# Sorting matrices of batches 1 to 3 built on VectorE, two heads at a time, instead of on GpSimd

## The chip, the cores and the metric

The kernel runs on one core of a Trainium2 chip. A core has TensorE (PE in the profile) for matrix products, VectorE (DVE), ScalarE (ACT) and GpSimd (POOL) for elementwise work, SyncE (SP), which here only issues transfers, and 16 DMA engines between its memory (SBUF) and the chip's main memory. PE writes to a second, small memory, PSUM, from which VectorE or ScalarE must copy its results. The metric is the device time of one execution in microseconds (us).

## The reference

Two stages are chained: a block-sorting attention, and a feed-forward network on its output. Shapes: q, k and v are 4 batches x 8 heads x 768 tokens x 64; `sort_net` has an 8 x 8 matrix for each batch and head.

```python
P = sort_net
for _ in range(5):
    P = exp(P - max(P, -1));  P = P / sum(P, -1);  P = P / sum(P, -2)
k_sorted = einsum('bhij,bhjcd->bhicd', P, k_blocks)     # 8 blocks of 96 tokens
v_sorted = einsum('bhij,bhjcd->bhicd', P, v_blocks)
attn = softmax(q_blocks @ k_sorted_blocks.T / 8)        # inside each block only
x = (attn @ v_sorted_blocks)  ->  3072 tokens x 512
h = maximum(x @ w_in, 0)                                # 512 -> 2048
out = (h * h) @ w_out                                   # 2048 -> 512
```

So each sorted block is a mixture of the head's 8 blocks, with the weights of one row of P.

## The kernel before

**Loads.** All inputs come through transfers that GpSimd issues (line 212), each of which converts to bf16: first the parts of batch 0, then the weights `w_in` and `w_out` in four quarters each, then q, k and v of batch 1 in two halves of four heads. The loads of batches 2 and 3 stand behind PE's last reads of batches 0 and 1, whose buffers they take.

**Sorting matrices.** The 768 tokens of a head lie on 128 partitions with 6 tokens each, so that a block is 16 partitions. The mixture of blocks is then a matrix product with a 128 x 128 matrix: P of the head, each entry spread over a 16 x 16 diagonal. These matrices of all 32 heads lie in `w_all` (128 partitions, 32 heads x 8 x 16, bf16). `build_w` (lines 323 to 335) writes those of `n` heads in one instruction, as the product of a 0/1 mask and the entries of P that `pt` holds, spread over the partitions (128 x 8 x 32). The entries of all batches are there once the Sinkhorn steps are done, at about 14 us. The eight heads of batch 0 are built on VectorE in three instructions (lines 621, 624, 625). The heads of batches 1 to 3 are built on GpSimd, with one instruction of eight heads for each batch (lines 626 and 627).

**Attention.** A unit of work is two heads of one batch; batch 0 is done in two halves of four blocks, the others whole. The stages of a unit: `s_q` transposes q on PE (line 361); `s_sort` makes the sorted K and then V as products with `w_all` (403), which are copied from PSUM by ScalarE or VectorE (line 166 or 168, tiles `ksT` and `vsT`); `s_sc` makes the scores (439) and their exponentials on ScalarE (455); `s_vt` transposes the sorted V (472), copied to `vs`; `s_av` makes the product of exponentials and V (499), which VectorE divides by the sums (508, 509); `s_xt` transposes the result (531) into `xT`, the network's input.

**Network.** Eight units of 384 tokens: 16 chunks of the up-projection (562), each with a ReLU on ScalarE (570) and a square on VectorE (573), then 12 chunks of the down-projection (590; four for each block of 128 tokens), each block copied and stored (605, 606).

**Order.** The order of the instructions on PE, VectorE and ScalarE is fixed ahead of time by a planner in the kernel's own program (`Plan`, lines 43 to 108). Each operation has an estimated cost, a list of operations that it depends on, and for attention on PE a due time, counted in network chunks. The planner goes through time, and takes for each engine what can start first; on equal terms it takes what was added first, and the network's operations are added last. Copies from PSUM may go to ScalarE or VectorE, whichever ends earlier by the estimates. PE has two queues, attention and network, and takes network chunks where the attention is not due or not ready. The planner's dependences order the instructions; on the chip an instruction waits only for the data that it uses. GpSimd's instructions keep the planner's order as well. Rotating PSUM slots (`Ring`, lines 26 to 40) limit how far PE runs ahead: two slots for sorts, scores and products with V together, three for the network, one for the transposes.

Of the kernel before, what the change touches and what calls it, by code (L numbers as in the profile page):

```python
# [111 lines left out]
def kernel(  # L112
# [10 lines left out]
    nc = tc.nc  # L123

    B, H, S, D = q.shape
# [27 lines left out]
    plan = Plan()  # L153
# [4 lines left out]
    def cost_f(n):  # L158
        return (0.17 + 0.82e-3 * n, 0.15 + 1.04e-3 * n)
# [4 lines left out]
    def copy(eng, out, in_):  # L164
        if eng == "ACT":
            nc.scalar.copy(out=out, in_=in_)  # L166
        else:
            nc.vector.tensor_copy(out=out, in_=in_)  # L168
# [89 lines left out]
    pt = const.tile([128, NB, NH], BF16)  # L258
# [61 lines left out]

    built = {}

    def build_w(h0, n, src, dep, eng="DVE"):
        def fn(e):
            s = tiles["pt"] if src is None else src
            (nc.gpsimd if eng == "POOL" else nc.vector).tensor_tensor(
                out=w_all[:, h0:h0 + n, :, :],
                in0=mask[:, None, None, :].to_broadcast([128, n, NB, C0]),
                in1=s[:, :, h0:h0 + n].rearrange("p i h -> p h i")[:, :, :, None]
                .to_broadcast([128, n, NB, C0]),  # L330
                op=ALU.mult)
        op = plan.add(eng, 0.15 + 0.134 * n, fn, [dep])
        for h in range(h0, h0 + n):
            built[h] = op
        return op
# [15 lines left out]
    def s_q(b, hp, p0, p1, due=0, after=None):  # L351

        n = p1 - p0
        t = {}

        def mm(e):
            qb = qkv[b][0]
            t["p"] = ps1.tile([128, NA, n], BF16, tag="p1", name="qtp")
            for a in range(NA):
                for h in range(2):  # L360
                    nc.tensor.transpose(  # L361
                        out=t["p"][64 * h:64 * (h + 1), a, :],
                        in_=qb[p0:p1, 2 * hp + h, D * a:D * (a + 1)],
                        identity=ident[p0:p1, p0:p1])
            if p0 == 0:
                tiles["qT", b, hp] = att.tile(
                    [128, NB, NA, C0], BF16, tag="qT", name="qT", bufs=6)

        def ev(e):
            copy(e, tiles["qT", b, hp][:, p0 // C0:p1 // C0, :, :],  # L370
                 t["p"].rearrange("p a (i c) -> p i a c", c=C0))

        if b == 0:
            dep = landed[b, 0, 0, p0]
        else:
            dep = landed[b, 0, HP * (2 * hp // HP), 0]
        s1, old = r1.take()
        if p0 == 0:
            qTs[b, hp], oldq = rqT.take()
        else:  # L380
            oldq = []
        pe = plan.add("PE", 0.1 + 0.002 * n, mm, [dep, after, id_op] + old, due)
        readers[b].append(pe)
        op = plan.add(AD, cost_b(NA * n), ev, [pe] + oldq)
        r1.use(s1, pe, op)
        rqT.use(qTs[b, hp], op)
        return op

    def s_sort(u, t, due=0, early=False):

        st = {}

        def mm(e):
            src = qkv[u.b][t]
            if early:
                tp = psf.tile([128, 512], FP32, tag="pf", name="tp")
                tp = tp[:, 0:NA * u.ni * C0].rearrange("p (a x) -> p a x", a=NA)
            else:
                tp = ps2.tile([128, NA, u.ni * C0], FP32, tag="p2", name="tp")
            st["p"] = tp  # L400
            for a in range(NA):
                for h in range(2):
                    nc.tensor.matmul(  # L403
                        out=tp[64 * h:64 * (h + 1), a, :],
                        lhsT=src[:, 2 * u.hp + h, D * a:D * (a + 1)],
                        rhs=w_all[:, H * u.b + 2 * u.hp + h, u.i0:u.i0 + u.ni, :]
                        .rearrange("p i c -> p (i c)"),
                        start=True, stop=True)

        def ev(e):  # L410
            h0 = u.halves[0]
            copy(e, (u.ksT if t == 1 else u.vsT)[:, h0:h0 + len(u.halves), 0:HS]
                 .rearrange("p h (x a) -> p h x a", a=NA),
                 st["p"].rearrange("p a (h x) -> p h x a", x=NQ * C0))

        h0 = 2 * u.hp
        dep = landed[u.b, t, h0 if u.b == 0 else HP * (h0 // HP), 0]
        ring = rf if early else r2
        s2, old = ring.take()
        pe = plan.add("PE", 0.385 if u.full else 0.27, mm,  # L420
                      [dep, built[H * u.b + h0], built[H * u.b + h0 + 1]] + old, due)
        readers[u.b].append(pe)
        op = plan.add(AD, cost_f(NA * C0 * u.ni), ev, [pe] + u.old)
        ring.use(s2, pe, op)
        return op

    def s_sc(u, due=0):

        u.exps = {}
        u.et, last = {}, []  # L430
        for hf in u.halves:
            st = {}

            def mm(e, hf=hf, st=st):
                qT = tiles["qT", u.b, u.hp]
                st["p"] = scp = ps2.tile([128, 2, 512], FP32, tag="p2", name="scp")
                for n in range(NQ):
                    for h in range(2):
                        nc.tensor.matmul(  # L439
                            out=scp[:, h, BLK * n:BLK * (n + 1)],  # L440
                            lhsT=u.ksT[64 * h:64 * (h + 1), hf, BLK * n:BLK * n + 128],
                            rhs=qT[64 * h:64 * (h + 1), NQ * hf + n, :, :]
                            .rearrange("p a c -> p (a c)"),
                            start=True, stop=True)

            s2, old = r2.take()
            u.et[hf], olde = ret.take()
            pe = plan.add("PE", 0.25, mm, [u.k_op, u.q_op] + old, due)
            r2.use(s2, pe)
            rqT.use(qTs[u.b, u.hp], pe)  # L450
            last.append(pe)
            u.exps[hf] = []
            for h in range(2):
                def ex(e, h=h, st=st, et=et_r[u.et[hf]]):
                    nc.scalar.activation(  # L455
                        out=et[:, h, 0:HS].rearrange("p (n c a) -> p n c a", c=C0, a=NA),
                        in_=st["p"][0:96, h, 0:HS].rearrange("p (n a c) -> p n c a", c=C0, a=NA),
                        func=AF.Exp, scale=scale)
                op = plan.add("ACT", cost_f(HS)[0], ex, [pe] + olde)
                r2.use(s2, op)  # L460
                u.exps[hf].append(op)
        u.sc_pe = last
# [154 lines left out]
    op = plan.add("DVE", 0.18, lambda e: nc.vector.tensor_copy(out=p_ij, in_=tiles["pT"]), [pe])  # L617
    r1.use(s1, pe, op)
    sf, old = rf.take()
    pe = plan.add("PE", 0.3, p_spread, [op] + old)  # L620
    w0 = build_w(0, 2, None, pe)
    cp = plan.add("ACT", 0.37, lambda e: nc.scalar.copy(out=pt, in_=tiles["pt"]), [pe])
    rf.use(sf, pe, w0, cp)
    build_w(2, 2, pt, cp)
    build_w(4, 4, pt, cp)
    for b in range(1, B):
        build_w(H * b, H, pt, cp, "POOL")

    us = []
    for n in range(HP + 3):  # L630
        if n < HP:
            u = Unit(0, n, (0,))
# [12 lines left out]
    n_up = NT + 4 * (HS // 128)  # L645
    todo = []

    def lay(b, halves, c0, c1):
        step = (c1 - c0) / (HP + 0.9)
        for hp in range(HP):  # L650
            c = c0 + step * hp
            box = {}

            def open_(due, b=b, hp=hp, box=box):
                u = box["u"] = Unit(b, hp, halves)
                u.q_op = s_q(b, hp, C0 * u.i0, C0 * (u.i0 + u.ni), due)
                u.k_op = s_sort(u, 1, due)
                u.v_op = s_sort(u, 2, due)

            for f, s in ((0.0, open_),  # L660
                         (0.35, lambda due, box=box: s_sc(box["u"], due)),
                         (0.5, lambda due, box=box: s_vt(box["u"], due)),
                         (0.75, lambda due, box=box: s_av(box["u"], due)),
                         (1.2, lambda due, box=box: s_xt(box["u"], due))):
                todo.append((c + step * f, len(todo), s, b))

    lay(0, (1,), 0, n_up)
    for b, (c0, c1) in enumerate(((n_up, 2 * n_up), (2 * n_up, 4 * n_up), (4 * n_up, 6 * n_up)), 1):
        lay(b, (0, 1), c0, c1)
# [49 lines left out]
```

## Time and profile before

| | |
|---|---|
| time, median of 3 runs | 248.12 us (246.68, 248.12, 248.26) |
| profiled execution's own time | 248.26 us |
| its span, first to last instruction | 246.3 us |
| PE busy | 234.4 us, 95% of the span |
| VectorE busy | 125.0 us, 51% |
| ScalarE busy | 122.3 us, 50% |
| GpSimd busy | 33.0 us, 13% |
| mean granted clock of TensorE | 0.984 of full speed |

The page of the profile shows, among other things, the busy tenths of each engine in 40 equal slices of the span, with the clock that TensorE was granted. Views of the trace answer in more detail: the list of who waited for whom, the timeline of one engine, the busy times in chosen stretches, the instructions of one source line with their shortest, median and longest duration, and the transfers with the time from issue to landing. Busy shares are averages over stages with different limits; a wait is put down to the operation that came last by the profile.

### The profile page before, as it was taken

The page shows a single profiled execution, that of the slowest core. Times are in us where ns is not written, and L with a number is a line of the kernel's source. Part 1 is how long each engine was busy: PE and PEld are TensorE (multiplying, and loading weights), DVE is VectorE, ACT ScalarE, POOL GpSimd, SP SyncE. Part 2 cuts the span into 40 slices and gives each one's busy share as a digit, 9 for nine tenths or more (in the row PEclk, how much of TensorE's full clock was granted, in tenths as well). Part 3 has the DMA queues.
Part 4 walks back from the last instruction along what each step waited for, and adds up shares of the span by engine and source line. Part 5 has one row for each costly group of instructions (what it writes and reads, how often), then busy time and mean ns, then how long its engine had stood idle before and what let it go on. Part 6 is the DMA issues. An engine that isn't in the chain of part 4 may idle for free.

```text
span 246.3 us, 5876 instructions
## 1 busy us (share of the span) xinstructions
PE 234.4 (95%) x2501; PEld 139.2 (57%) x2501; DVE 125.0 (51%) x311; ACT 122.3 (50%) x255; POOL 33.0 (13%) x44
## 2 busy tenths in 40 slices
PE   7999974999999999999999999999999999999993
PEld 2777642555666656655566456655566456446541
DVE  6677787632787434855286306835387115204400
ACT  4365642523787607762467218642567047417510
POOL 8843373150000700000000000000000000000000
PEclk9999995999999999999999999999999999999999
DMA  6999999999600799001110021001200120021012
GB/s 82 197 205 207 206 206 203 159 151 239 124 3 3 105 220 191 0 4 43 47 43 3 8 78 45 3 0 45 85 3 1 45 85 0 0 88 43 0 43 85
DMA packets 20488, 20.29 MB, mean 82 GB/s; under 512 B 1008, under 2 KB 17392, under 8 KB 20464
## 3 DMA queue, kind: packets, MB, share of 16 engines
q0 software_dynamic: 16960, 13.63, 35.8%
q1 hardware_dynamic: 3504, 6.30, 7.0%
q8 instruction: 19, 0.31, 0.5%
q14 instruction: 5, 0.04, 0.1%
HBM read 27.27 MB, written 6.29 MB: 136 GB/s over the span
## 4 chain that ended last, share of the span: by engine, by line
PE 92%; DVE 5%; ACT 1%; issue 0%
PE hp L562 35%; PE op L590 34%; PE tp L403 5%; PE qtp L361 3%; PE vbp L472 3%; PE scp L439 3%; PE oup L499 3%; PE fill L283 3%; DVE h L573 3%; PE xtp L531 2%; ACT qT L166 1%; DVE ao L509 1%; DVE vs L168 0%; ACT ob L166 0%; DVE ones L185 0%
## 5 line engine op out<-in xcount | busy, mean ns | idle before, releaser
L562 PE MATMUL hp<-xT,w_in_bf 128*128 128x384 bf16 x512 | 93.9, 329 | 0.0
L590 PE MATMUL op<-w_out_bf,h 128*128 128x512 bf16 x384 | 87.9, 379 | 0.0
L570 ACT ACTIVATE h<-hp 128x384 bf16<-128x384 f32 x128 | 62.3, 492 | 33.0 <-PE hp L562 27.7
L573 DVE TENSOR_TENSOR h<-h 128x384 bf16<-128x384 bf16 x128 | 50.4, 405 | 39.4 <-ACT h L570 38.7
L562 PEld LDWEIGHTS <-w_in_bf 128*128 128x128 bf16 x512 | 46.8, 98 | 28.7 <-issue 0.7
L590 PEld LDWEIGHTS <-h 128*128 128x128 bf16 x384 | 36.1, 98 | 39.7
L166 ACT COPY ob<-op 128x512 f32<-128x512 f32 x24 | 14.1, 586 | 57.5 <-PE op L590 57.5
L455 ACT ACTIVATE et<-scp 96x384 bf16<-96x384 f32 x64 | 26.4, 490 | 7.4 <-PE scp L439 7.4
L509 DVE TENSOR_TENSOR ao<-oup,rec 96x512 bf16<-96x512 f32 x32 | 22.0, 687 | 1.1
L168 DVE COPY vs<-vbp 96x1024 bf16<-96x1024 bf16 (+1 forms) x20 | 11.6, 580 | 19.5 <-PE vbp L472 19.4
L168 DVE COPY qT<-qtp 128x768 bf16<-128x768 bf16 (+1 forms) x14 | 6.8, 485 | 19.3 <-PE qtp L361 18.9
L168 DVE COPY xT<-xtp 128x768 bf16<-128x768 bf16 (+1 forms) x17 | 8.5, 499 | 14.7 <-PE xtp L531 14.2
L166 ACT CAST ksT<-tp 128x768 bf16<-128x768 f32 (+1 forms) x15 | 10.0, 670 | 9.5 <-PE tp L403 9.3
L283 PE MATMUL fill<-ones 128*128 128x128 bf16 (+1 forms) x108 | 13.1, 267 | 1.5 <-DVE ones L185 1.5
L403 PE MATMUL tp<-w_all,vb 128*64 128x128 bf16 (+1 forms) x240 | 9.2, 213 | 5.3 <-DVE ao L509 5.2
L499 PEld LDWEIGHTS <-et 96*128 96x128 bf16 x256 | 10.6, 98 | 2.6
L212 POOL DMA_DIRECT2D qb<-in_q_dram x8 | 6.1, 768 | 41.4 <-PE qtp L361 36.9
L499 PE MATMUL oup<-vs,et 96*128 96x65 bf16 x256 | 11.4, 193 | 0.0
L168 DVE CAST vsT<-tp 128x768 bf16<-128x768 f32 (+1 forms) x13 | 10.8, 831 | 0.8
L403 PEld LDWEIGHTS <-vb 128*64 128x64 bf16 x240 | 7.1, 113 | 6.4 <-DVE ao L509 5.4
L361 PEld LDWEIGHTS <-qb 128*64 128x64 bf16 (+1 forms) x240 | 6.9, 109 | 6.6 <-issue 5.9
L472 PE MATMUL vbp<-ident,vsT 128*128 128x128 bf16 x128 | 10.5, 219 | 0.0
(49 smaller groups left out, 134.8 us busy)
## 6 DMA issues: line engine op xcount, KB each, us to landing
out_dram<-ob SPq DMA_DIRECT2D x24, 256.0 KB, 2.0
qb<-in_q_dram POOLq DMA_DIRECT2D x8, 384.0 KB, 12.1
kb<-in_k_dram POOLq DMA_DIRECT2D x6, 384.0 KB, 9.8
vb<-in_v_dram POOLq DMA_DIRECT2D x6, 384.0 KB, 11.8
w_in_bf<-in_moe_w_in_dram POOLq DMA_DIRECT2D x4, 512.0 KB, 12.9
w_out_bf<-in_moe_w_out_dram POOLq DMA_DIRECT2D x4, 512.0 KB, 19.0
kb<-in_k_dram POOLq DMA_DIRECT2D x4, 192.0 KB, 6.2
vb<-in_v_dram POOLq DMA_DIRECT2D x4, 192.0 KB, 6.5
```

The source lines that it names most:

```text
L166: nc.scalar.copy(out=out, in_=in_)
L168: nc.vector.tensor_copy(out=out, in_=in_)
L283: nc.tensor.matmul(out=tiles["fill"][:, 0:w], lhsT=ones[:, 0:128], rhs=ones[:, 0:w], start=True, stop=True)
L403: nc.tensor.matmul(out=tp[64 * h:64 * (h + 1), a, :], lhsT=src[:, 2 * u.hp + h, D * a:D * (a + 1)], rhs=w_all[:, H * u.b + 2 * u.hp + h, u ...
L455: nc.scalar.activation(out=et[:, h, 0:HS].rearrange("p (n c a) -> p n c a", c=C0, a=NA), in_=st["p"][0:96, h, 0:HS].rearrange("p (n a c) - ...
L472: nc.tensor.transpose(out=vbp[:, n, :], in_=u.vsT[:, i // NQ, BLK * (i % NQ):BLK * (i % NQ) + 128], identity=ident)
L499: nc.tensor.matmul(out=oup[:, h, 66 * n:66 * n + D + 1], lhsT=et_r[u.et[hf]][:, h, BLK * n:BLK * n + 128], rhs=u.vs[:, NQ * hf + n, h, 0:D ...
L509: nc.vector.tensor_tensor(out=u.ao[:, n0:n0 + NQ, :, :].rearrange("p n e d -> p e n d"), in0=ov[:, :, :, 0:D], in1=rec[:, :, :, None].to_b ...
L562: nc.tensor.matmul(out=t["hp", nt][:, 0:HS], lhsT=w_in_bf[:, kc, 128 * nt:128 * (nt + 1)], rhs=xT[:, kc, t0:t0 + HS], start=(kc == 0), sto ...
L570: nc.scalar.activation(out=t["h1", nt], in_=t["hp", nt][:, 0:HS], func=AF.Relu)
L573: nc.vector.tensor_tensor(out=t["h2"][:, nt, :], in0=t["h1", nt], in1=t["h1", nt], op=ALU.mult)
L590: nc.tensor.matmul(out=t["op", mt], lhsT=t["h2"][:, nt, 128 * mt:128 * (mt + 1)], rhs=w_out_bf[:, nt, :], start=(nt == 0), stop=(nt == NT ...
```

## The change

`build_w` loses its choice of engine and always uses VectorE. The three builds of eight heads are gone. In their place the function that opens a unit of two heads in batch b > 0 adds a build of just these two heads, whose planner dependence is the sort of K of the same pair of heads in batch b - 1 (the operation that copies it from PSUM, kept in the new table `kops`). The planner's cost for two heads is 0.15 + 0.134 x 2 = 0.418 us. Twelve such builds arise: four pairs for each of batches 1, 2 and 3. For batch 1 the sort that counts is that of the second half of batch 0.

```diff
-    def build_w(h0, n, src, dep, eng="DVE"):
+    def build_w(h0, n, src, dep):
         def fn(e):
             s = tiles["pt"] if src is None else src
-            (nc.gpsimd if eng == "POOL" else nc.vector).tensor_tensor(
+            nc.vector.tensor_tensor(
                 out=w_all[:, h0:h0 + n, :, :],
...
-        op = plan.add(eng, 0.15 + 0.134 * n, fn, [dep])
+        op = plan.add("DVE", 0.15 + 0.134 * n, fn, [dep])
...
     build_w(4, 4, pt, cp)
-    for b in range(1, B):
-        build_w(H * b, H, pt, cp, "POOL")
...
+    kops = {}
+
     def lay(b, halves, c0, c1):
...
             def open_(due, b=b, hp=hp, box=box):
                 u = box["u"] = Unit(b, hp, halves)
                 u.q_op = s_q(b, hp, C0 * u.i0, C0 * (u.i0 + u.ni), due)
-                u.k_op = s_sort(u, 1, due)
+                if b > 0:
+                    build_w(H * b + 2 * hp, 2, pt, kops[b - 1, hp])
+                u.k_op = kops[b, hp] = s_sort(u, 1, due)
                 u.v_op = s_sort(u, 2, due)
```

## The prediction

> **What bounds the kernel now.** I read the page first: the span, the line of TensorE (PE) in the 40 slices, and the granted clock under it.
>
> ```profile
> span 246.3 us, 5876 instructions
> ...
> PE   7999974999999999999999999999999999999993
> ...
> PEclk9999995999999999999999999999999999999999
> ```
>
> A slice is 6.16 us. PE is full from the second slice to the last but one, except for slices six and seven (the 7 and the 4, 30.8 to 43.1 us), and in the second of these the clock is down to 5 tenths. So this is a PE-bound kernel with one hole. Next I asked who made PE wait between 24 and 200 us, and then read each engine's timeline around the hole: VectorE (DVE), GpSimd (POOL), and the statistics of the line that stands out.
>
> ```profile
> PE tp L403 <- DVE ao L509: 5.2, 1, 5.2
> ```
>
> ```profile
> 30.47 0.36 DVE L168 COPY xT<-xtp 128x384 bf16<-128x384 bf16 x1
> 30.82 0.36 DVE L573 TENSOR_TENSOR h<-h 128x384 bf16<-128x384 bf16 x1
> 31.64 0.36 DVE L573 TENSOR_TENSOR h<-h 128x384 bf16<-128x384 bf16 x1 [0.46 <-ACT h L570]
> 32.38 0.42 DVE L168 COPY vs<-vbp 96x512 bf16<-96x512 bf16 x1 [0.38 <-PE vbp L472]
> 32.78 6.76 DVE L573 TENSOR_TENSOR h<-h 128x384 bf16<-128x384 bf16 x1
> 39.46 0.19 DVE L508 RECIPROCAL rec<-oup 96x8 f32<-96x8 f32 x1
> 39.69 0.69 DVE L509 TENSOR_TENSOR ao<-oup,rec 96x512 bf16<-96x512 f32 x1
> ```
>
> ```profile
> 18.10 0.74 POOL L212 DMA_DIRECT2D w_out_bf<-in_moe_w_out_dram  x1 [2.37 <-DMA w_in_bf<-in_moe_w_in_dram]
> ...
> 32.64 0.74 POOL L212 DMA_DIRECT2D qb<-in_q_dram  x1 [1.82 <-DMA w_out_bf<-in_moe_w_out_dram]
> 33.39 5.92 POOL L326 TENSOR_TENSOR w_all<-mask,pt 128x1024 bf16<-128x1024 bf16 x3
> ```
>
> ```profile
> L573 DVE TENSOR_TENSOR h<-h x128: 343/358/6760, 25.8 to 232.5; 128x384 bf16<-128x384 bf16 x128
> ```
>
> The first of these is the whole list of PE's waits from 24 to 200 us: one wait, 5.2 us. Columns of a timeline are start, duration (us), engine, line, operation. One square (L573) holds VectorE for 6.76 us; the last row has minimum, median and maximum of all 128 squares in ns: 358 is usual, 6760 happened once. It ends at 32.78 + 6.76 = 39.54, and the three GpSimd instructions that build the sorting matrices of batches 1 to 3 end at 33.39 + 5.92 = 39.31. These three are what the change removes. Behind the square stand the reciprocal and the division (L509) that empty a PSUM tile of probabilities times V; the next sort of V on PE takes that slot and waits for them. This is one coincidence in time, not proof, and one thing speaks against it: the square's record starts 0.61 us before GpSimd's.
>
> **What the removal gives.** The idle time is not the whole price, since the clock went down too.
>
> ```profile
> 37.00:38.00 1.00, 0.00 (x0) 0.00 (x0) 1.00 (x1) 0.00 (x0) 1.00 (x2) 0.58 1.32 204
> 43.00:44.00 1.00, 1.00 (x7) 0.27 (x7) 0.34 (x2) 0.01 (x1) 0.00 (x0) 0.51 1.33 205
> 44.00:45.00 1.00, 1.00 (x15) 0.66 (x14) 0.36 (x1) 1.00 (x3) 0.00 (x0) 1.00 1.29 200
> ```
>
> After each stretch and its length stand the busy times of PE, weight loads, DVE, ACT and POOL; the first of the last three columns is the granted clock: half from 37 to 44 us. To price hole and slow clock together I compare PE with itself. The unit before does the same steps in the same order (transposes of Q, sort of K, sort of V, an up-projection chunk, transposes of the attention output, a chunk, scores). First and last step of both, from PE's timeline:
>
> ```profile
> 28.63 0.38 PE L361 MATMUL qtp<-ident,qb 64*64 64x64 bf16 x12
> ...
> 31.02 0.34 PE L439 MATMUL scp<-qT,ksT 64*128 64x96 bf16 x8
> ...
> 34.50 0.38 PE L361 MATMUL qtp<-ident,qb 64*64 64x64 bf16 x12
> 34.81 0.38 PE L403 MATMUL tp<-w_all,kb 128*64 128x64 bf16 x12
> 40.43 0.53 PE L403 MATMUL tp<-w_all,vb 128*64 128x64 bf16 x12 [5.25 <-DVE ao L509]
> ...
> 43.89 0.37 PE L439 MATMUL scp<-qT,ksT 64*128 64x96 bf16 x8
> ```
>
> 31.02 - 28.63 = 2.39 us against 43.89 - 34.50 = 9.39 us: the stall costs 7.0 us, 5.25 of them idle and the other 1.75 slow clock. PE waits for nothing else up to 200 us and its order is fixed, so all that stands behind moves up by 7.0 us, if its inputs are there. Loads do not move up with it, so I checked the two that could be late next: each one's time to landing, from the DMA view of the stretch around its issue, and PE's first use.
>
> ```profile
> w_out_bf<-in_moe_w_out_dram POOLq DMA_DIRECT2D x1, 512.0 KB, 19.6
> ```
>
> ```profile
> qb<-in_q_dram POOLq DMA_DIRECT2D x1, 384.0 KB, 16.7
> ```
>
> ```profile
> 46.66 1.03 PE L590 MATMUL op<-w_out_bf,h 128*128 128x512 bf16 x4
> ```
>
> ```profile
> 59.23 0.53 PE L361 MATMUL qtp<-ident,qb 128*64 128x128 bf16 x12
> ```
>
> The last quarter of w_out is issued at 18.10 and lands 19.6 us later, at 37.7; the first down-projection moves from 46.66 to 39.7. The last load of batch 1 is issued at 32.64 and lands at 49.3; batch 1 begins at 59.2 now, 52.2 then. Margins of 2.0 and 2.9 us. The three builds stand in GpSimd's queue behind all loads of batch 1 and ahead of those of batch 2, which wait for PE's last transposes of batch 0 anyway and go out with them, 7 us earlier.
>
> **What the addition costs.** Twelve builds of two heads on VectorE. Both engines' builds as they are now, with minimum, median and maximum in ns:
>
> ```profile
> L326 POOL TENSOR_TENSOR w_all<-mask,pt x3: 1994/2002/2016, 33.4 to 37.3; 128x1024 bf16<-128x1024 bf16 x3
> L326 DVE TENSOR_TENSOR w_all<-mask,pt x2: 424/554/685, 14.0 to 14.4; 128x256 bf16<-128x256 bf16 x1, 128x512 bf16<-128x512 bf16 x1
> ```
>
> Two heads are the 256-element form, 0.424 us; 12 x 0.424 = 5.09 us of VectorE, four builds in each of the second half of batch 0, batch 1 and batch 2. Their dependence on the sort of K one batch earlier exists only in the planner: it fixes the place in VectorE's order, while the operands (mask, pt) are ready since 14 us, so a build itself waits for nothing. The use comes a batch later, so PE does not wait for a build either. What is left is that whatever is queued behind one on VectorE comes up to 0.42 us later.
>
> ```profile
> 24.00:33.00 9.00, 9.00 (x137) 5.79 (x138) 6.33 (x17) 6.16 (x14) 2.58 (x4) 1.00 1.24 208
> 59.00:94.00 35.00, 35.00 (x486) 22.06 (x484) 21.49 (x46) 21.18 (x44) 4.46 (x6) 1.00 0.63 108
> 94.00:146.00 52.00, 52.00 (x527) 30.82 (x522) 27.33 (x64) 27.31 (x57) 0.00 (x0) 1.00 0.14 42
> ```
>
> PE is busy throughout these stretches, VectorE (third busy time) 70%, 61% and 53%. Tightest is the first, where one build would fall at about 30 us. Behind it the square at 30.82 and what follows would be late, but 0.46 us of idle stand before the square at 31.64 and another 0.38 before the copy of V at 32.38, the first one on which PE depends closely (its product with the probabilities follows at once). These two hide the 0.42 us; if that cover is gone, the build costs PE 0.42 us. The bounds: 0 us (the change only adds work to VectorE, and PE has no second wait from which a gain could come) and 5.1 us (every build in full on PE's path). The nearest row is the list of waits: with 17, 46 and 64 VectorE instructions in these stretches, PE waited for none of them, so the value is near the low end. I take 0.4 us, one build of twelve, for what the planner's other order may spill.
>
> **The sum.** The profiled execution took 248.26 us: the span of 246.3 and 1.96 around it. It is 0.14 above the median of 248.12. 248.26 - 7.0 + 0.4 = 241.7 us.
>
> **The rivals.**
>
> *The builds cost in full.* VectorE becomes PE's limit, because each build delays a copy that frees PSUM: 248.26 - 7.0 + 5.1 = 246.4. For it: copies like the one at 32.38, with PE close behind. Against it: the busy shares above, and PE's one wait. In part, with six to eight builds on the path (2.5 to 3.4 us): 243.8 to 244.7.
>
> *Only a third of the stall goes.* One GpSimd instruction takes 2.0 us, and the square was held through three. If only the first held it, and the remainder has a cause that stays, the gain is 2.0 us: 248.26 - 2.0 + 0.4 = 246.7. Against it: the square ends 0.2 us after the third. The Trainium skill, SBUF — State Buffer, section "SBUF: two separate sides", says that a VectorE instruction with two SBUF inputs and a GpSimd instruction that reads SBUF take turns at a shared pair of ports, whichever is first keeping it for one whole instruction. By that rule the square would be let in after one of the three, as in this rival, and the time would be its 246.7; the trace's 6.76 us does not agree.
>
> *The square is long for a reason of VectorE's own, and stays long: slower.* Then the 7.0 us stay, PE waits for VectorE at this place as before, and each build that lands on the path adds its 0.424 us: 248.26 + 5.1 = 253.4 with all twelve, and slower by 1% (2.5 us) from six on. For it: the 0.61 us by which the square starts early. Against it: 127 of 128 squares are short, and the long one is the one that meets GpSimd's builds.
>
> *The work is not moved*, with GpSimd still building: 248.3. Nothing in the diff points there.
>
> **How the numbers follow.** A measurement of this kernel can tell about 1% (2.5 us) from no change. The forecast gets 0.86, with a range of its own from 239.7 to 243.4: upwards five builds on the path (2.1 us over 241.3, the sum without builds), downwards the 1.6 us by which the fastest run shown (246.68) lies under the profiled one. Builds at a price beyond that get 0.07, of which 0.06 is the partial case, still faster by over 1%: the bound of 245.6 is reached at ten builds. The third of a stall gets 0.04, the slower one 0.02, no move 0.01. Faster: 0.86 + 0.06 = 0.92; same: 0.01 + 0.04 + 0.01 = 0.06; slower: 0.02. The range goes from 239.7 to 244.5, up to nearly eight builds on the path.
>
> **What would show it.** The maximum of the squares near 360 ns; no large GpSimd instruction; the clock at 9 tenths in slice seven; PE's list of waits from 24 us on empty or with entries of some tenths; twelve more builds of 424 ns on VectorE; the first down-projection near 39.7 us, batch 1 near 52.2. I am wrong if one square is still several us long, if PE's waits for VectorE add up to more than 2 us, or if a load ends a wait of PE at the down-projection or at batch 1.

## The result

The changed kernel takes 241.27 us (median of four, 241.0 to 241.77) against 248.01 for the kernel before, which was timed with it: a ratio of 0.9739, with a 95% interval from 0.9705 to 0.9772. The forecast was 241.7 us. The profiled execution took 241.0 us with a span of 238.9. A profile is of one execution and not always of a typical one: 241.0 us is the lowest of these four and the 248.26 of before the highest of its four, and below gp_spare_x3 and before_with_waits were profiled in their longest execution (248.12 and 248.67 us), gp_spare_x1 and gp_spare_x2 in their shortest (241.69 and 243.81 us).

The page of the changed kernel, for the three lines shown of before:

```profile
span 238.9 us, 5867 instructions
...
PE   7899999999999999999999999999999999999993
...
PEclk9999999999999999999999999999999999999999
```

The hole in slices six and seven is closed, and the clock stays at 9 tenths. The list of PE's waits between 24 and 200 us, and the squares' line with shortest, median and longest duration in ns:

```profile
PE op L590 <- issue: 0.3, 2, 0.2
PE oup L499 <- DVE vs L168: 0.2, 1, 0.2
```

```profile
L573 DVE TENSOR_TENSOR h<-h x128: 343/358/359, 25.2 to 225.2; 128x384 bf16<-128x384 bf16 x128
```

The 5.2 us wait is gone, two small entries are new, and no square is long. (The two waits of the first entry stand at 108 and 162 us, where records of the down-projection seem to be missing from the trace: the page has 368 of its 384 matrix products.) VectorE's timeline where the long square stood, and the builds there, by duration in ns:

```profile
31.79 0.42 DVE L168 COPY vs<-vbp 96x512 bf16<-96x512 bf16 x1 [0.38 <-PE vbp L472]
32.19 0.36 DVE L573 TENSOR_TENSOR h<-h 128x384 bf16<-128x384 bf16 x1
32.72 0.20 DVE L508 RECIPROCAL rec<-oup 96x8 f32<-96x8 f32 x1 [0.17 <-PE oup L499]
32.95 0.69 DVE L509 TENSOR_TENSOR ao<-oup,rec 96x512 bf16<-96x512 f32 x1
33.56 0.69 DVE L573 TENSOR_TENSOR h<-h 128x384 bf16<-128x384 bf16 x2
34.33 0.36 DVE L168 COPY qT<-qtp 128x384 bf16<-128x384 bf16 x1
34.60 0.35 DVE L573 TENSOR_TENSOR h<-h 128x384 bf16<-128x384 bf16 x1
34.87 0.42 DVE L326 TENSOR_TENSOR w_all<-mask,pt 128x256 bf16<-128x256 bf16 x1
35.75 0.36 DVE L168 COPY xT<-xtp 128x384 bf16<-128x384 bf16 x1 [0.46 <-PE xtp L531]
```

```profile
L326 DVE TENSOR_TENSOR w_all<-mask,pt x14: 415/416/684, 13.5 to 121.4; 128x256 bf16<-128x256 bf16 x13, 128x512 bf16<-128x512 bf16 x1
```

The division (L509) follows the copy of V after 1.2 us, where it was 7.3 us before. A build (34.87) is followed by 0.46 us in which VectorE waits for PE.

To see where the time went I compare four places that both traces have: PE's first sort, the first transposes of Q in the second half of batch 0, the first of batch 1, and the end. From PE's timeline, first the kernel before, then the changed one:

```profile
13.66 0.38 PE L403 MATMUL tp<-w_all,kb 128*64 128x64 bf16 x12
...
23.61 0.37 PE L361 MATMUL qtp<-ident,qb 64*64 64x64 bf16 x12 [0.17 <-DVE xT L168]
```

```profile
13.07 0.38 PE L403 MATMUL tp<-w_all,kb 128*64 128x64 bf16 x12
...
23.02 0.38 PE L361 MATMUL qtp<-ident,qb 64*64 64x64 bf16 x12 [0.17 <-DVE xT L168]
...
51.61 0.53 PE L361 MATMUL qtp<-ident,qb 128*64 128x128 bf16 x12
```

| stretch | before | after | difference |
|---|---|---|---|
| to the first sort | 13.66 | 13.07 | -0.59 |
| first sort to second half of batch 0 | 9.95 | 9.95 | 0 |
| from there to batch 1 (59.23 and 51.61) | 35.62 | 28.59 | -7.03 |
| batch 1 to the end of the span | 187.07 | 187.29 | +0.22 |

The first stretch holds nothing that was changed, and it differs by as much between two traces of one kernel: before_again, below, has its first sort at 14.20. 7.03 of the 7.4 us come from the stretch with the long square, which after the change also holds the four builds for batch 1. In the last stretch stand the eight builds for batches 2 and 3. Its 0.22 us are as long as the second new entry in the list of waits, in PE's timeline and in VectorE's:

```profile
63.30 0.41 PE L499 MATMUL oup<-vs,et 96*128 96x65 bf16 x8 [0.22 <-DVE vs L168]
```

```profile
62.46 0.69 DVE L168 COPY vs<-vbp 96x1024 bf16<-96x1024 bf16 x1 [0.94 <-PE vbp L472]
```

Ahead of this copy VectorE itself waited 0.94 us for PE, so no build made it late. The wait belongs to the new order that the planner made: all six traces with this order have it, with 187.29 to 187.35 us in the last stretch, and none of the eight with another order has it (187.56 us in gp_pieces_x12, whose mean clock was 0.75 in the last 4.2 us, and 186.97 to 187.07 in the others).

### The profile page after: what moved, and what is told of

It reads as the page before. It is cut to its first block, busy times and chain, and to the rows that moved or that the text cites. A ratio compares the mean times of both kernels' runs of the same rounds, so it can differ in the third digit from the quotient of the medians.

```text
span 238.9 us, 5867 instructions
## 1 busy us (share of the span) xinstructions
PE 230.5 (96%) x2485; PEld 138.1 (58%) x2501; DVE 121.4 (51%) x322; ACT 123.0 (51%) x256; POOL 27.0 (11%) x41
## 4 chain that ended last, share of the span: by engine, by line
PE 91%; DVE 4%; ACT 2%; issue 1%; POOL 0%; POOLq 0%
PE hp L562 35%; PE op L590 34%; PE tp L403 5%; PE vbp L472 3%; PE qtp L361 3%; PE oup L499 3%; PE scp L439 3%; PE xtp L531 3%; ACT qT L166 1%; DVE p_sb L266 1%; PE fill L283 0%; DVE vs L168 0%; ACT h L570 0%; DVE rs L265 0%; POOL qb L212 0%
## 5 line engine op out<-in xcount | busy, mean ns | idle before, releaser
L562 PE MATMUL hp<-xT,w_in_bf 128*128 128x384 bf16 x512 | 92.8, 326 | 0.0
L590 PE MATMUL op<-w_out_bf,h 128*128 128x512 bf16 x368 | 86.2, 379 | 1.0 <-issue 0.3
L573 DVE TENSOR_TENSOR h<-h 128x384 bf16<-128x384 bf16 x128 | 43.9, 354 | 37.2 <-ACT h L570 36.7
L590 PEld LDWEIGHTS <-h 128*128 128x128 bf16 x384 | 36.1, 98 | 39.7
L509 DVE TENSOR_TENSOR ao<-oup,rec 96x512 bf16<-96x512 f32 x32 | 22.0, 687 | 1.1
L168 DVE COPY qT<-qtp 128x768 bf16<-128x768 bf16 (+1 forms) x15 | 7.3, 489 | 18.9 <-PE qtp L361 18.4
L166 ACT CAST ksT<-tp 128x768 bf16<-128x768 f32 (+1 forms) x17 | 11.7, 686 | 9.9 <-PE tp L403 9.6
L168 DVE COPY xT<-xtp 128x768 bf16<-128x768 bf16 (+1 forms) x16 | 7.9, 496 | 13.3 <-PE xtp L531 12.8
L283 PE MATMUL fill<-ones 128*128 128x128 bf16 (+1 forms) x108 | 12.0, 255 | 1.5 <-DVE ones L185 1.5
L168 DVE CAST vsT<-tp 128x768 bf16<-128x768 f32 (+1 forms) x14 | 11.8, 840 | 0.8
L508 DVE RECIPROCAL rec<-oup 96x8 f32<-96x8 f32 x32 | 6.4, 199 | 8.3 <-PE oup L499 8.1
L361 PE MATMUL qtp<-ident,qb 128*64 128x128 bf16 (+1 forms) x240 | 9.3, 212 | 0.8 <-DVE qT L168 0.4
```

The source lines that it names most:

```text
L283: nc.tensor.matmul(out=tiles["fill"][:, 0:w], lhsT=ones[:, 0:128], rhs=ones[:, 0:w], start=True, stop=True)
L361: nc.tensor.transpose(out=t["p"][64 * h:64 * (h + 1), a, :], in_=qb[p0:p1, 2 * hp + h, D * a:D * (a + 1)], identity=ident[p0:p1, p0:p1])
L509: nc.vector.tensor_tensor(out=u.ao[:, n0:n0 + NQ, :, :].rearrange("p n e d -> p e n d"), in0=ov[:, :, :, 0:D], in1=rec[:, :, :, None].to_b ...
L562: nc.tensor.matmul(out=t["hp", nt][:, 0:HS], lhsT=w_in_bf[:, kc, 128 * nt:128 * (nt + 1)], rhs=xT[:, kc, t0:t0 + HS], start=(kc == 0), sto ...
L573: nc.vector.tensor_tensor(out=t["h2"][:, nt, :], in0=t["h1", nt], in1=t["h1", nt], op=ALU.mult)
L590: nc.tensor.matmul(out=t["op", mt], lhsT=t["h2"][:, nt, 128 * mt:128 * (mt + 1)], rhs=w_out_bf[:, nt, :], start=(nt == 0), stop=(nt == NT ...
```

## Experiments

All times are medians; a ratio is to the kernel before timed with the run.

| run | what it is | us | ratio (95% interval) | longest square |
|---|---|---|---|---|
| no_builds | no builds for batches 1 to 3 | 241.0 | 0.971 (0.9695 to 0.9725) | short |
| gp_spare_x3 | change, and 3 spare GpSimd products, each waiting for the last | 245.3 | 0.9894 (0.9859 to 0.9929) | 2.46 us |
| gp_spare_x2 | the same with 2 | 245.31 | 0.9895 (0.9846 to 0.9943) | 2.15 us |
| gp_spare_x1 | the same with 1 | 242.89 | 0.9811 (0.9766 to 0.9856) | 2.03 us |
| gp_spare_no_waits | with 3, none waiting | 248.18 | 1.000 (0.9975 to 1.0025) | 5.84 us |
| gp_memset_x3 | change, and 3 spare GpSimd memsets | 241.24 | 0.9743 (0.9702 to 0.9785) | 0.36 us |
| before_again | before, unchanged | 248.2 | 1.0017 (0.9991 to 1.0043) | 6.75 us |
| before_with_waits | before, each GpSimd build waiting for the last | 245.64 | 0.9926 (0.9894 to 0.9958) | 3.02 us |
| gp_pieces_x6 | before, GpSimd builds of 4 heads | 248.78 | 1.0035 (1.0018 to 1.0053) | 6.51 us |
| gp_pieces_x12 | GpSimd builds of 2 heads | 241.3 | 0.9728 (0.9704 to 0.9752) | 0.84 us |
| gp_later | GpSimd builds of 8 heads, 9 us later | 240.72 | 0.9725 (0.9687 to 0.9763) | 0.36 us |
| dve_at_once | all built on VectorE at 14 us | 243.27 | 0.9789 (0.9766 to 0.9812) | short |

### Do the builds on VectorE cost anything?

```diff
-    for b in range(1, B):
-        build_w(H * b, H, pt, cp, "POOL")
+    for h in range(H, NH):
+        built[h] = built[h % H]
...
-                        rhs=w_all[:, H * u.b + 2 * u.hp + h, u.i0:u.i0 + u.ni, :]
+                        rhs=w_all[:, 2 * u.hp + h, u.i0:u.i0 + u.ni, :]
```

> Left out: the sorting matrices of batches 1 to 3 are not built at all; these batches use the matrices of batch 0. GpSimd and VectorE lose the work altogether. Theory (the gain is the stall, and the twelve VectorE builds are hidden): 240.9 to 241.4 us, at most 0.4 below the changed kernel's 241.27, no square over 0.4 us. Rival (builds partly on PE's path): 0.8 us or more below it, so under 240.5.

Measured 241.0 us, 0.3 below the changed kernel and inside the first expectation. The stall does not need a replacement to vanish, and twelve builds of 0.42 us, 5 us of VectorE, cost at most some tenths. From batch 1 to the end this trace has 187.04 us (52.16 to 239.2), as the kernel before (187.07), and from the second half of batch 0 to batch 1 it has 28.60, as the changed kernel (28.59).

### Is it GpSimd that holds the square?

Spare work on the changed kernel, at the place in GpSimd's order where the builds stood; three instructions here, two and one in the other runs:

```diff
     build_w(4, 4, pt, cp)
+    scr = const.tile([128, H, NB, C0], BF16, name="scr")
+    def extra(e):
+        nc.gpsimd.tensor_tensor(
+            out=scr, in0=mask[:, None, None, :].to_broadcast([128, H, NB, C0]),
+            in1=pt[:, :, 0:H].rearrange("p i h -> p h i")[:, :, :, None]
+            .to_broadcast([128, H, NB, C0]),
+            op=ALU.mult)
+    for _ in range(3):
+        plan.add("POOL", 1.22, extra, [cp])
```

> The changed kernel, with GpSimd still doing three instructions of the old shape at the old place, reading the same tiles and writing to a spare tile that nobody reads. Theory (GpSimd's elementwise work holds the square): one square of 6 to 7 us again, 5 us of PE idle, the clock halved, 247.5 to 249 us. Rival (the square was long for a reason of VectorE's own or of the old order): no long square, 241 to 241.8 us.

> With two spare GpSimd instructions. Theory: a square of 4 to 4.8 us, PE idle 3 to 3.6 us, 244 to 246 us, with the upper half of this if the clock is halved too. Rival (only the first instruction holds it): as with one.

> As the run with three spare GpSimd instructions, with one. Theory (the square is shut out for as long as GpSimd works): one square of about 2 to 2.8 us, PE idle 1 to 1.6 us, no halved clock, 242 to 243 us. Rival (only the first instruction of a row holds the square, the remainder of the old stall had another cause): the same 242 to 243 here, so this run prices one instruction and is read against those with two and three.

Work that nobody uses brings back a good part of the loss: 4.0 us over the changed kernel with three, 4.0 with two, 1.6 with one. So the square is long because of GpSimd. But only the times with two and one came as expected: with three, no square of 6 to 7 us came back, and with two, none of 4 to 4.8, but two of 1.82 and 2.15 us one after the other. PE's waits were shorter than expected too: 2.2 us with two (I had said 3 to 3.6) and 0.6 us with one (1 to 1.6). VectorE's timeline of gp_spare_x1 and of gp_spare_x3, each with GpSimd's row behind it:

```profile
33.70 2.31 DVE L573 TENSOR_TENSOR h<-h 128x384 bf16<-128x384 bf16 x2
```

```profile
33.49 2.02 POOL L629 TENSOR_TENSOR scr<-mask,pt 128x1024 bf16<-128x1024 bf16 x1
```

```profile
33.33 2.46 DVE L573 TENSOR_TENSOR h<-h 128x384 bf16<-128x384 bf16 x1
35.71 0.19 DVE L508 RECIPROCAL rec<-oup 96x8 f32<-96x8 f32 x1
35.94 0.69 DVE L509 TENSOR_TENSOR ao<-oup,rec 96x512 bf16<-96x512 f32 x1
36.54 3.39 DVE L573 TENSOR_TENSOR h<-h 128x384 bf16<-128x384 bf16 x2
```

```profile
33.55 6.17 POOL L629 TENSOR_TENSOR scr<-mask,pt 128x1024 bf16<-128x1024 bf16 x3
```

With one, the first of two squares ends 0.22 us after GpSimd (33.70 + 2.03 against 33.49 + 2.02). With three, the first square is let in after GpSimd's first instruction, a reciprocal and a division pass at their usual 0.19 and 0.69 us while GpSimd works, and the next squares wait again, one GpSimd instruction each (1.32 and 2.15 us). That is the rival "only a third goes" in its mechanism, one instruction at a time. It left open why the kernel before held one square through all three. The spare instructions write the same tile, and so each waits for the last on a semaphore; the old builds did not. That is the difference that the next runs change.

### One instruction, or the whole row?

```diff
-    scr = const.tile([128, H, NB, C0], BF16, name="scr")
+    scrs = [const.tile([128, H, NB, C0], BF16, name=f"scr{i}") for i in range(3)]
...
+    for i in range(3):
+        plan.add("POOL", 1.22, lambda e, i=i: extra(e, i), [cp])
```

> As the run with three spare GpSimd instructions, which wrote one tile and so waited for each other; here each writes a tile of its own and none waits, as in the kernel before. Theory after the first runs (GpSimd keeps the square out through a whole row of instructions that are issued without a wait between them, and lets it in after each where they wait): one hold of 5 to 6.8 us, 4 us or more of PE idle, halved clock, 246.5 to 249 us. Rival (it is one instruction at a time, and the 6.76 us of the kernel before were chance or another cause): holds of 2.5 us at most, 244 to 245.8 us.

And the other way round, the kernel before with overlapping builds, so that each waits; and the kernel before as it was:

```diff
-        build_w(H * b, H, pt, cp, "POOL")
+        build_w(H * b, H + (b < B - 1), pt, cp, "POOL")
```

> The kernel before, with its first two GpSimd builds writing nine heads instead of eight, so that each overlaps the next by one head and the next one waits for it; the output is the same. Theory: holds of at most 2.6 us each instead of one of 6.76, 244 to 246.5 us. Rival (the waits do not matter): one hold of about 7 us, 248 to 249 us.

> The kernel before, unchanged, for a second trace. If the hold through all three instructions is how this order works: one square of 6 to 7 us again. If it is chance: holds of 2 to 2.5 us, or another number of them.

The theory held in all three. gp_spare_no_waits:

```profile
34.06 6.11 DVE L573 TENSOR_TENSOR h<-h 128x384 bf16<-128x384 bf16 x2
```

```profile
33.76 5.92 POOL L629 TENSOR_TENSOR scr<-mask,pt 128x1024 bf16<-128x1024 bf16 x3
```

before_with_waits, and before_again:

```profile
32.77 3.02 DVE L573 TENSOR_TENSOR h<-h 128x384 bf16<-128x384 bf16 x1
...
35.94 0.69 DVE L509 TENSOR_TENSOR ao<-oup,rec 96x512 bf16<-96x512 f32 x1
36.55 3.62 DVE L573 TENSOR_TENSOR h<-h 128x384 bf16<-128x384 bf16 x2
```

```profile
33.33 6.75 DVE L573 TENSOR_TENSOR h<-h 128x384 bf16<-128x384 bf16 x1
```

Without waits in between, three GpSimd instructions take 5.92 us from the start of the first to the end of the last, a little under three times 2.0, each starting 0.05 us before the one ahead ends, and a square stays out for the whole row: 5.84 and 6.75 us. With waits they take 6.17 us, with some 0.08 us between two, and the square gets in after the first. (In before_with_waits two are an eighth longer, for the ninth head, 2.24 us, and the square's record starts 0.56 us ahead of the first: hence 3.02 us, where I had said at most 2.6.) In time: 248.18 against 245.3 for the spare work, and 245.64 against 248.2 for the old builds. An added semaphore wait between GpSimd instructions made the kernel before 0.7% faster. Whether it is the wait itself that lets the square in, or the 0.08 us without a GpSimd instruction that comes with it, these runs do not tell.

### The size of the pieces

```diff
-                    build_w(H * b + 2 * hp, 2, pt, kops[b - 1, hp])
+                    build_w(H * b + 2 * hp, 2, pt, kops[b - 1, hp], "POOL")
```

> The builds back on GpSimd at the old place, but in twelve instructions of two heads (about 0.5 us each) in a row. If VectorE and GpSimd change places after each instruction: squares of at most 1 us, PE idle under 1 us, 241 to 242.5 us. If whoever waits on VectorE stays shut out until GpSimd's row ends: one square of 6 to 7 us and 247.5 to 249 us.

```diff
-    for b in range(1, B):
-        build_w(H * b, H, pt, cp, "POOL")
+    for h0 in range(H, NH, 4):
+        build_w(h0, 4, pt, cp, "POOL")
```

> The kernel before, with GpSimd building in six instructions of four heads (about 1.1 us each, none waiting for another) instead of three of eight. Twelve of two heads let a square in after each one; three of eight shut it out for the whole row. If the row shuts out as with three: one square of 5 to 7 us, 247 to 249 us. If it changes hands as with twelve: squares of at most 1.5 us, PE idle under 1 us, 241 to 242.5 us.

Here GpSimd builds again (in the first, `build_w` has its choice of engine back), in a row without waits. (The kernel's call of `manual_schedule` fixes the planner's order for PE, VectorE and ScalarE alone. In the trace the twelve stand in one row at the old place, ahead of the loads of batch 2, although the planner had spread them one batch ahead of their use. So what is said above of GpSimd keeping the planner's order is wrong.)

```profile
33.57 1.42 DVE L573 TENSOR_TENSOR h<-h 128x384 bf16<-128x384 bf16 x2
34.92 0.34 DVE L168 COPY qT<-qtp 128x384 bf16<-128x384 bf16 x1
35.18 0.52 DVE L573 TENSOR_TENSOR h<-h 128x384 bf16<-128x384 bf16 x1
```

```profile
33.37 8.36 POOL L326 TENSOR_TENSOR w_all<-mask,pt 128x256 bf16<-128x256 bf16 x12
```

```profile
33.58 6.78 DVE L573 TENSOR_TENSOR h<-h 128x384 bf16<-128x384 bf16 x2
```

```profile
33.53 6.34 POOL L326 TENSOR_TENSOR w_all<-mask,pt 128x512 bf16<-128x512 bf16 x6
```

The first two fences are gp_pieces_x12, the others gp_pieces_x6. Twelve pieces of about 0.74 us cost VectorE a few tenths per square and PE nothing: 241.3 us, the time of the change, with all work still on GpSimd and 8.36 us of it. Six pieces of 1.08 us shut a square out for the whole row, 6.51 us, and cost as much as three of 2.0. So the absence of a wait is not the whole rule: below some length between 0.74 and 1.08 us (two and four heads) a square gets in between pieces. Why is open; the records show no gap between the pieces of two heads either (each starts 0.02 to 0.04 us before the one ahead ends).

### What on GpSimd, and what on VectorE

```diff
+    scr = const.tile([128, 2048], FP32, name="scr")
+    def extra(e):
+        nc.gpsimd.memset(scr, 0.0)
...
+        plan.add("POOL", 1.22, extra, [cp])
```

> The changed kernel, with three GpSimd memsets of 2048 fp32 elements at the old place: GpSimd writes a spare tile and reads nothing. Rule of the Trainium skill, SBUF — State Buffer, section SBUF: two separate sides (a VectorE instruction with two SBUF inputs is blocked only by a GpSimd instruction that reads SBUF): no long square, 241 to 241.8 us. Rival (any GpSimd work on SBUF holds it): a square as long as the memsets, and PE idle for that less about 1.3 us.

```diff
-                in0=mask[:, None, None, :].to_broadcast([128, n, NB, C0]),
+                in0=(mask if m is None else m)[:, None, None, :].to_broadcast([128, n, NB, C0]),
...
+                if b == 1 and hp == 0:
+                    m2 = plan.add("ACT", 0.25, lambda e: nc.scalar.copy(out=mask2, in_=mask),
+                                  [kops[0, HP - 1]])
+                    for bb in range(1, B):
+                        build_w(H * bb, H, pt, m2, "POOL", mask2)
```

> Batches 1 to 3 built on GpSimd as before, three instructions of eight heads, but about 8 us later: they read a copy of the mask that ScalarE makes after the last sort of batch 0, so they run from about 41 to 48 us, where VectorE has only copies out of PSUM and no squares. Theory (only VectorE instructions with both inputs in SBUF are shut out): copies keep 0.36 to 0.7 us, no PE idle, 241 to 241.8 us. Rival (GpSimd's work holds any VectorE instruction): a copy or division of several us and 1 to 5 us more.

```profile
33.69 5.55 POOL L629 MEMSET scr<- 128x2048 f32 x3
```

```profile
L573 DVE TENSOR_TENSOR h<-h x128: 343/357/359, 25.7 to 225.7; 128x384 bf16<-128x384 bf16 x128
```

5.55 us of memsets in the same place leave every square alone (241.24 us). This is what the Trainium skill, SBUF — State Buffer, section "SBUF: two separate sides", states: a VectorE instruction with two SBUF inputs is blocked only by a GpSimd instruction that reads SBUF. Its other half, that the lock is for one instruction, agrees with the runs that have waits (squares of 1.3 to 3.0 us) and not with the rows of three and of six that have none (5.84 to 6.75 us).

gp_later, GpSimd and then VectorE:

```profile
42.18 5.94 POOL L326 TENSOR_TENSOR w_all<-mask,pt 128x1024 bf16<-128x1024 bf16 x3
```

```profile
43.54 0.42 DVE L168 COPY vs<-vbp 96x512 bf16<-96x512 bf16 x1 [1.11 <-PE vbp L472]
45.52 0.20 DVE L508 RECIPROCAL rec<-oup 96x8 f32<-96x8 f32 x1 [1.56 <-PE oup L499]
45.76 0.69 DVE L509 TENSOR_TENSOR ao<-oup,rec 96x512 bf16<-96x512 f32 x1
47.42 0.36 DVE L168 COPY xT<-xtp 128x384 bf16<-128x384 bf16 x1 [0.98 <-PE xtp L531]
```

The same three instructions, same engine, same row without waits, 9 us later, where the network is in its down-projection and has no squares: all copies and divisions out of PSUM keep their time, and the kernel takes 240.72 us. That is 0.3 us under the range I had given. Its ratio's interval and that of the change (0.9739, 0.9705 to 0.9772) overlap, so the times alone do not tell that it is better. Its trace does not have the change's 0.22 us wait (186.97 us from batch 1 to the end).

### All on VectorE at once

```diff
-        build_w(H * b, H, pt, cp, "POOL")
+        build_w(H * b, H, pt, cp)
```

> All of batches 1 to 3 built on VectorE at 14 us, three instructions of eight heads (about 1.2 us each), instead of two heads at a time one batch ahead. Theory (what counts is that GpSimd does not do it, and that the work does not stand on a path): the stall is gone as in the change, but 3.7 us of VectorE stand in the start, where PE waits for copies: 242 to 245 us. Rival (the place on VectorE does not matter): 241 to 241.6 us.

```profile
14.41 4.43 DVE L326 TENSOR_TENSOR w_all<-mask,pt 128x256 bf16<-128x256 bf16 x5 [0.44 <-ACT pt L622]
```

243.27 us, inside the theory's range and 2.0 us over the change. In VectorE's timeline five builds stand in one piece from 14.41 (two for batch 0, three for the others), at a time when PE waits for its copies. From the first sort to the second half of batch 0 this trace has 11.23 us (14.02 to 25.25) against 9.95: 1.3 us for some 3.4 us of builds (4.43 less 1.03 for the two of batch 0 as before); the planner gives copies to ScalarE instead. Another 0.95 us of its profiled span lies ahead of the first sort (14.02 against 13.07), where nothing was changed and where the other traces lie between 13.08 and 14.21; from batch 1 to the end it has 0.24 us less than the change. So the builds explain 1.3 of the 2.0 us, and the remainder is not shown to be theirs.

## Why the prediction was right

*The stall, 7.0 us.* Right. The steps that took 9.39 us before the change, from the transposes of Q at 34.50 to the scores at 43.89, take 2.39 us after it, as the unit ahead of them did already:

```profile
33.91 0.38 PE L361 MATMUL qtp<-ident,qb 64*64 64x64 bf16 x12
...
36.30 0.34 PE L439 MATMUL scp<-qT,ksT 64*128 64x96 bf16 x8
```

The wider stretch of the table has 7.03. Comparing PE with itself over equal steps took in the slow clock that the list of waits (5.2 us) leaves out. That GpSimd was the cause was argued there from one coincidence; the spare work shows it.

*The builds, 0.4 us.* Right in kind, and a little high: nothing up to batch 1 (28.59 us against 28.60 in no_builds), 0.2 us from there on, and 0.3 us between the medians of the change and of no_builds. The 0.4 stood for what the planner's other order may spill, and the 0.2 are that: one wait, and not one behind a build. The duration was 0.416 us against 0.424. VectorE's idle time hid the builds, as said. (Two of them fell between 24 and 33 us, at 24.41 and 29.43, where one was counted.)

*What is late next.* Nothing was. The first down-projection starts at 39.04 (39.7 forecast) and batch 1 at 51.61 (52.2), both early by the 0.6 us that came in before the first sort. But the margins were smaller than forecast, 1.1 and 1.3 us in place of 2.0 and 2.9: the last quarter of w_out was issued at 18.36 and took 19.6 us, the last load of batch 1 was issued at 33.15 and took 17.2.

*The sum.* 248.26 - 7.03 + 0.22 - 0.59 is 240.9, beside the profiled 241.0. The -0.59 was not in the forecast and is not the change's: the changed instructions begin later. It makes most of the distance from 241.7, and that part of the miss is chance. By the medians the gain is 6.74 us (248.01 - 241.27), where the forecast has 6.6 from its base of 248.26.

*The rivals.* The builds in full (246.4) and the slower one (253.4) are refuted by no_builds and by the spare work. "Only a third of the stall goes" was wrong for this kernel, in which GpSimd's row had no waits, but its mechanism is real: before_with_waits has it.

*The objection,* that the square's record starts 0.61 us before GpSimd's, came back in before_again (33.33 and 33.94), and there the hold is GpSimd's. In gp_spare_no_waits the square starts after GpSimd (34.06 and 33.76) and is held as well. What the 0.61 us are was not settled.

## What to carry to other kernels

If a VectorE instruction with both inputs in SBUF is once many times as long as its median, look for GpSimd instructions that read SBUF beside it, and price the hole with the slow clock in it, by the same steps of the bottleneck engine elsewhere. Moving the work to VectorE's idle time removes the hold, but so does moving it on GpSimd to a stage without such instructions, or cutting it into short pieces: all three gave the same time here.

## What the hardware showed that was not expected

A row of GpSimd products without waits between them kept VectorE's squares out for the whole row (6.75 us through three of 2.0 us, 6.51 us through six of 1.08 us), but not a row of twelve of 0.74 us, and not a row with semaphore waits between them. The clock fell to half during PE's waits: in the kernel before (a wait of 5.2 us), before_again (5.2), gp_pieces_x6 (5.1) and gp_spare_no_waits (4.4) it fell 2.0 to 3.4 us after PE had stopped, and it came back 6.8 us later in each. In gp_spare_x3 it fell only 0.4 us into a wait of 2.4 us, with a wait of 0.9 us and 1.1 us of work ahead of it. In the profiled execution of gp_spare_x2 it stayed full through a wait of 2.2 us; but the other three executions of that kernel have a mean granted clock of 0.992 to 0.993, so in them it fell for a while, though no trace shows where. One wait's length alone does not tell. Nor is the price of a stall one number: of 57 timings of the kernel before beside these runs (one of 473.4 us is left aside), 20 have a mean granted clock of 0.993 and a median of 247.15 us, and 36 have 0.982 to 0.986 and 248.33 us. The 7.0 us belong to the latter.

```profile
PE xtp L531 <- DVE qT L168: 2.4, 1, 2.4
PE tp L403 <- DVE ao L509: 0.9, 1, 0.9
```

```profile
38.00:39.00 1.00, 0.00 (x0) 0.00 (x0) 1.00 (x1) 0.44 (x1) 1.00 (x1) 0.63 1.32 203
```

The first two lines are from the list of PE's waits in gp_spare_x3, the third its busy times from 38 to 39 us, with the granted clock at 0.63, third from the end.
